# An attention and gMLP kernel: two attention products held at other places in VectorE's order

## The chip, the cores and the metric

The kernel runs on one core of a Trainium2 chip. The metric is the device time of one execution in microseconds (us), as the median of several runs. The engines of a core are TensorE (PE, matrix products; PEld is its loading of weights), VectorE (DVE), ScalarE (ACT), GpSimd (POOL) and SyncE (SP, which issues DMAs). Each runs its own instructions strictly in the order in which the built program lists them, and waits on semaphores where it needs another engine's result.

## The reference

The input x has 2048 rows of 512 numbers. Its normalised rows go through an attention branch and a gated MLP branch:

```
xn = layernorm(x)
# attention: 32 heads of 16, each row sees 8 rows at distance 0, 2, .. 14 behind it
q, k, v = split(xn @ wqkv)
s = softmax(q . k[i - 2w] / 4) weighted sum of v[i - 2w], heads joined, @ wo
# gMLP: 1792 hidden, halves of 896
z  = gelu(xn @ w_in);  z1 = z[:, :896];  z2 = layernorm(z[:, 896:])
g  = w_sp @ z2 + b_sp          # w_sp is 2048 x 2048, it mixes rows
b  = (z1 * g) @ w_out
out = x + s * silu(b)
```

All is float32. A float32 matrix product is done as three passes of a reduced type: every operand is split into a high part (a copy on ACT) and a low part (the difference, on DVE), and high x high, high x low and low x high are added up in PSUM.

## The kernel before, in words

On PE the work runs in stages, one behind the other: the q, k, v product (lines 385 to 387), z1 (703 to 705), z2 (730 to 732), the spatial product g (825), the projection with w_out (tiles b, 1066 to 1068), and the projection with wo (tiles s, the same lines). The trace shows these stages back to back from some 12 to 689 us.

The **spatial product** mixes rows with w_sp. It is computed by a scheme with seven block products on sums of blocks; `block_product` (848) runs one of them over eight steps, and in each step takes the next 128 x 512 mixing weight and multiplies it with up to four tiles of z2. The accumulators are the eight PSUM banks g_a_f. `plain` (859) hands out the weights that are blocks of w_sp as they stand, named wsp_c_js. Each is loaded, and then split by `split` (194): the high part on ACT at line 195, the low part on DVE at line 197. The list `lows` holds all low parts in the order in which they were written, so `lows[-1]` is the latest. In the names of the trace, wsp_1h is the high part of the second weight and wsp_1l its low part; the trace leaves the first number out. The banks g_1_f are first set to a bias by `seed` on ACT (line 843), behind a matmul at line 983.

In the **z2 stage**, the tiles zt come out of gelu on ACT (733). DVE takes their statistics (742, 743, 745), POOL raises the variance to the power -1/2 (746) and makes the negative shift nmz (748), and ACT normalises with it (754). DVE then forms differences and sums of the tiles (767), which the block products need, and splits them (197, tiles BIG<-zt).

The **attention** between the projections is done on DVE in 32 steps (16 units of rows and heads, two steps each), written as one chain in `attention`, lines 530 to 686. Each step has scores pr<-k,q (573), their sum over the head's 16 numbers, lg<-pr (580), the softmax (shift 598 to 601, exponential on ACT 606, norm 612 to 614), the **weighted product** pv<-v,lg (620), a first fold of it on POOL (633), two more folds and a transposition on DVE (638, 639, 646), and a store of the result to o_d by POOL's queue (647). POOL's queue also loads k, q and v. `line` (536) ties each DVE instruction of the attention to the one before it, so that their order among themselves never changes. The weighted products are kept in the list `sums_of` (628): the tenth is pv_4_4, the eleventh pv_5_0, and the twenty-fifth pv_12_0.

The order of the whole program is chosen when it is built: a scheduler goes through the program with a model of how long each instruction takes and always places what its model finds ready, the attention with a low priority (LOW, 532). Lines that call `add_manual_dep` with NOSYNC tie one instruction behind another in this order; they add no wait at run time. One such line stands in `plain`: when the weight wsp_0_6 is handed out, a weighted product is put behind its low part.

`wout` (1054) lists the seven split weights of w_out, wout_0 to wout_6. `upper_last` (961) evicts the last accumulators of g through the tiles yl, and `late` (930) loads and splits products stored earlier (tiles ul).

The attention's results come back from o_d into the tiles ol, are split (o_3h on ACT, o_3l on DVE), and multiplied with wo in the last stage; line 1117 is silu on tiles sg, line 1127 multiplies it with the result.

Of the kernel before, what the change touches and what calls it, by code (L numbers as in the profile page):

```python
# [52 lines left out]
NOSYNC = mybir.DependencyInfo(mybir.DependencyClass.NoSync, mybir.DependencyReason.DATA)  # L53
# [4 lines left out]
def kernel(  # L58
# [15 lines left out]
    lows, highs, sums_of = [], [], []  # L74
# [85 lines left out]
    def weight_pair(name):  # L160
        i = next(slot)
        return (
            wts.tile([P, 512], F32R, tag=f"whi{i}", name=name + "h"),
            wts.tile([P, 512], F32R, tag=f"wlo{i}", name=name + "l"),
        )

    def fetch(src, n, name):
        raw = raws.tile([P, 512], F32, tag="raw", name=name + "r", bufs=RAW)
        pin(nc.sync.dma_start(raw[:, :n], src))
        return raw  # L170
# [4 lines left out]
    def prep(src, n, name, raw=None, pair_=None):  # L175
        if raw is None:
            raw = fetch(src, n, name)
        hi, lo = pair_ or weight_pair(name)
        split(hi[:, :n], lo[:, :n], raw[:, :n])
        return hi, lo  # L180
# [13 lines left out]
    def split(hi, lo, src):  # L194
        first_ = pin(nc.scalar.activation(hi, src, AF.Copy))
        highs.append(first_)
        lows.append(pin(nc.vector.tensor_tensor(lo, src, hi.bitcast(F32), op=ALU.subtract)))
        return first_
# [94 lines left out]
    first = []  # L293
# [230 lines left out]
    def t4(name, n=2):  # L524
        t = wide.tile([P, 2 * CT], F32, tag="t4", name=name, bufs=WIDE)
        return t.rearrange("p (i t) -> p i t", i=2)[:, :n]
# [208 lines left out]
    def spatial_block(c, js):  # L735
        return prep(w_sp[c, js], CT, f"wsp_{c}_{js}")
# [95 lines left out]
    def z1_pair(c, f0, n):  # L832
        zl = t4(f"zl_{c}_{f0}", n)
        nc.sync.dma_start(zl, z1_d[f0 : f0 + n, c].rearrange("f p t -> p f t"))
        return zl
# [12 lines left out]
    def block_product(a, name, z, w, odd=None, start=False, stop=False, steps=()):  # L848
        for n, s0 in enumerate(range(0, HT, 2)):
            for s in (s0, s0 + 1):  # L850
                wp = w(s)
                for f in range(ODD):
                    three(banks[a, f], z(s, f), wp, start and s == 0, s == HT - 1, not start)
                if odd:
                    three(banks[a, ODD], odd(s), wp, False, s == HT - 1, True)
            for do in steps[n] if steps else ():
                do()

    def plain(a, c, r):
        def w(s):  # L860
            js = r * HT + s
            pair_ = spatial.get((2 * a + c, js)) or spatial_block(2 * a + c, js)
            if (a, c, js) == (0, 0, 6):
                tc.add_manual_dep(
                    sums_of[9].ins, lows[-1].ins.name, NOSYNC, reason="first weights ahead"
                )
            return pair_

        return w

    def summed(a, half_, i):
        return lambda s: prep(sums_d[a, half_, s, :, i], CT, f"ws_{a}{half_}{i}_{s}")
# [12 lines left out]
    def at(r, f0):  # L885
        return lambda s, f: z2_block(r * HT + s, f0 + f)
# [9 lines left out]
    def minus(out_, p_, q_):  # L896
        nc.vector.tensor_tensor(out_, p_, q_, op=ALU.subtract)
# [28 lines left out]
    def gated(c, f, src, zt):  # L926
        times(zt, src, zt)
        split(*ut_at(c, f), zt)
# [32 lines left out]
    def upper_last(a, f0, n):  # L961
        zl, yl = z1_pair(2 * a, LAST + f0, n), t4(f"yl_{a}_{f0}", n)
        nc.sync.dma_start(yl, y_d[a, f0 : f0 + n].rearrange("f p t -> p f t"))
        for f in range(f0, f0 + n):
            minus(yl[:, f - f0], banks[a, f], yl[:, f - f0])
            gated(2 * a, LAST + f, yl[:, f - f0], zl[:, f - f0])
# [85 lines left out]
    upper_last(0, 2, 1)  # L1052
    block_product(1, "m3b", at(1, LAST), summed(1, 1, 0))
    wout = [prep(w_out[:, f, :], D, f"wout_{f}") for f in range(FB)]
    upper_last(1, 0, 2)
    upper_last(1, 2, 1)
    for a in range(2):
# [120 lines left out]
```

## Time and profile before

| what | value |
|---|---|
| time, median of 3 runs (lowest, highest) | 695.79 us (694.64, 697.7) |
| the profiled execution's own time | 694.39 us |
| its span in the trace | 692.4 us |
| matmuls in the profiled execution | 3084 |
| bytes moved by DMA | 182.36 MB, mean 263 GB/s |

The profile is of one execution; its instructions span 692.4 us, and 1.99 us of the execution's own time lie around them. Here the busy share of PE and DVE in 40 equal slices of the span, in tenths (9 is 90% or more), and the clock granted to PE:

```profile
PE   8999999999999999999999999999999999999998
DVE  6677867999999979899999999999999999979775
PEclk9999999999999999999999999999999999999999
```

Both engines are busy nearly throughout. In rows of the timeline that follow below, the columns are the start, the duration, the engine, the line, the operation, result and operands, and in brackets the idle time before it and who ended it. In rows of groups they are the count, the busy time and the mean of one in ns, and the idle time before.

### The profile page before, as it was taken

How to read it: one execution, taken by the hardware profiler on the slowest of the kernel's cores; microseconds unless marked ns; L12 is line 12 of the kernel's file. 1: busy time of each engine (PE TensorE's matmuls, PEld its weight loads, DVE VectorE, ACT ScalarE, POOL GpSimd, SP SyncE). 2: the span in 40 equal slices, each digit the busy share in tenths (PEclk: the TensorE clock that was granted, in tenths of full speed). 3: DMA queues.
4: the chain of work that ended last, by engine and by line, in shares of the span. 5: the costliest groups of instructions: out<-in, count | busy, mean ns of one | idle time of the engine just before them, and what ended most of it. 6: DMA issues, size and time to landing. Idle time of an engine off the chain costs nothing.

```text
span 692.4 us, 9239 instructions
## 1 busy us (share of the span) xinstructions
PE 686.6 (99%) x3084; PEld 573.6 (83%) x3084; DVE 619.5 (89%) x866; ACT 278.6 (40%) x458; POOL 214.0 (31%) x242
## 2 busy tenths in 40 slices
PE   8999999999999999999999999999999999999998
PEld 7788888888888899987888888888888888888886
DVE  6677867999999979899999999999999999979775
ACT  3343233324324256765624544433344353211531
POOL 3104737282343321223223221223201202632320
PEclk9999999999999999999999999999999999999999
DMA  8769899969999865266998778776585791645896
GB/s 268 245 199 297 276 353 370 344 213 336 411 410 384 334 222 186 92 216 218 287 401 299 277 241 294 228 251 223 161 290 196 234 339 65 214 159 191 251 324 238
DMA packets 102223, 182.36 MB, mean 263 GB/s; under 512 B 9184, under 2 KB 45280, under 8 KB 102176
## 3 DMA queue, kind: packets, MB, share of 16 engines
q1 hardware_dynamic: 56624, 102.21, 44.2%
q0 software_dynamic: 13824, 52.24, 20.9%
q10 hardware_dynamic: 31728, 27.33, 11.7%
q8 instruction: 24, 0.39, 0.2%
q14 instruction: 23, 0.19, 0.1%
HBM read 122.42 MB, written 59.32 MB: 262 GB/s over the span
## 4 chain that ended last, share of the span: by engine, by line
PE 93%; DVE 2%; DMA 1%; ACT 1%; issue 1%; POOL 1%; SPq 0%; DVEq 0%; ACTq 0%
PE g L825 37%; PE qkv L385 6%; PE qkv L387 6%; PE qkv L386 6%; PE z L705 4%; PE z L703 4%; PE b L1068 4%; PE b L1066 4%; PE b L1067 4%; PE z L704 4%; PE z L732 3%; PE z L731 3%; PE z L730 3%; PE s L1068 2%; PE s L1067 2%; PE s L1066 2%
## 5 line engine op out<-in xcount | busy, mean ns | idle before, releaser
L633 POOL TENSOR_TENSOR pv<-pv 128x1024 f32<-128x1024 f32 x29 | 69.6, 2401 | 92.8 <-DVE pv L620 82.5
L573 DVE TENSOR_TENSOR pr<-k,q 128x2048 f32<-128x2048 f32 x32 | 73.6, 2299 | 4.3 <-DMA k<-qkv_d 4.1
L620 DVE TENSOR_TENSOR pv<-v,lg 128x2048 f32<-128x2048 f32 x32 | 74.5, 2329 | 0.6
L580 DVE TENSOR_REDUCE lg<-pr 128x128 f32<-128x2048 f32 x32 | 72.9, 2279 | 0.1
L647 POOL DMA_DIRECT2D o_d<-tt x32 | 18.0, 563 | 137.8 <-DVE tt L646 104.6
L433 ACT ACTIVATE stage<-qkv 128x512 f32<-128x512 f32 x40 | 23.0, 590 | 30.9 <-DMA qkv_d<-stage 21.0
L1077 ACT ACTIVATE bt<-b 128x512 f32<-128x512 f32 x16 | 9.6, 599 | 50.0 <-PE b L1068 45.8
L807 POOL DMA_DIRECT2D ol<-o_d x32 | 17.8, 556 | 36.2 <-DMA ol<-o_d 9.1
L709 ACT ACTIVATE z1t<-z 128x512 f32<-128x512 f32 x28 | 15.5, 596 | 27.5 <-DMA z_d<-z1t 14.5
L732 PE MATMUL z<-w_0h,BIG 128*128 128x512 f32 x64 | 25.0, 391 | 0.0
L731 PE MATMUL z<-w_0l,BIG 128*128 128x512 f32 x64 | 25.0, 391 | 0.0
L730 PE MATMUL z<-w_0h,BIG 128*128 128x512 f32 x64 | 24.9, 389 | 0.0
L742 DVE BATCH_NORM_STATS2 zst<-zt 128x6 f32<-128x448 f32 x32 | 19.3, 613 | 6.1 <-ACT zt L733 6.0
L754 ACT ACTIVATE zt<-zt,nmz,mvz 128x896 f32<-128x896 f32 x16 | 17.5, 1129 | 17.1 <-POOL nmz L748 17.1
L280 DVE TENSOR_TENSOR xT<-xT,mr 128x512 f32<-128x512 f32 x20 | 13.8, 688 | 11.8 <-DMA mr<-mv_d 6.8
L638 DVE TENSOR_TENSOR pv<-pv 128x512 f32<-128x512 f32 x32 | 22.9, 715 | 0.0
L732 PE MATMUL z<-w_1h,BIG 128*128 128x384 f32 x64 | 21.5, 336 | 0.0
L730 PE MATMUL z<-w_1h,BIG 128*128 128x384 f32 x64 | 21.5, 335 | 0.0
L731 PE MATMUL z<-w_1l,BIG 128*128 128x384 f32 x64 | 21.4, 335 | 0.0
L733 ACT ACTIVATE zt<-z 128x512 f32<-128x512 f32 (+1 forms) x32 | 15.9, 536 | 13.5 <-DMA sums_d<-sa 10.2
L552 POOL DMA_DIRECT2D k<-qkv_d x13 | 7.0, 536 | 43.8 <-DVE pr L573 43.8
L393 POOL TENSOR_TENSOR sb<-sa,sb 128x512 f32<-128x512 f32 x12 | 18.9, 1574 | 5.1 <-DMA sb<-in_w_sp 4.8
(478 smaller groups left out, 2256.9 us busy)
## 6 DMA issues: line engine op xcount, KB each, us to landing
qkv_d<-stage ACTq DMA_DIRECT2D x24, 512.0 KB
v<-qkv_d POOLq DMA_DIRECT2D x14, 704.0 KB, 5.1
k<-qkv_d POOLq DMA_DIRECT2D x13, 704.0 KB, 5.8
sums_d<-sa POOLq DMA_DIRECT2D x14, 512.0 KB, 7.9
sums_d<-sb POOLq DMA_DIRECT2D x14, 512.0 KB, 7.9
z_d<-z1t ACTq DMA_DIRECT2D x14, 512.0 KB
zl<-z_d SPq DMA_DIRECT2D x12, 512.0 KB
tr<-t_d SPq DMA_DIRECT2D x12, 384.0 KB
```

The lines of the kernel that those rows point to most:

```text
L385: nc.tensor.matmul(pq, xh[:, k], wh, start=k == 0, stop=False)
L386: nc.tensor.matmul(pq, xh[:, k], wl, start=False, stop=False)
L387: nc.tensor.matmul(pq, xl[:, k], wh, start=False, stop=k == KB - 1)
L573: line(nc.vector.tensor_tensor(pr, taps(ks[u], j0), qb.unsqueeze(1).to_broadcast([P, W, NJ * CS]), op=ALU.mult))
L580: line(nc.vector.tensor_reduce(lgs[u][:, j0 * HS : (j0 + NJ) * HS].rearrange("p i w -> p w i"), pr.rearrange("p w (i d) -> p w i d", d=DH) ...
L620: line(nc.vector.tensor_tensor(pv.rearrange("p w (i d) -> p w i d", d=DH), taps(vs[u], j0).rearrange("p w (i d) -> p w i d", d=DH), lgs[u] ...
L633: eng.tensor_tensor(pv[:, 0:4], pv[:, 0:4], pv[:, 4:8], op=ALU.add)
L730: nc.tensor.matmul(pz, xh[:, k], wh, start=k == 0, stop=False)
L731: nc.tensor.matmul(pz, xh[:, k], wl, start=False, stop=False)
L732: nc.tensor.matmul(pz, xl[:, k], wh, start=False, stop=k == KB - 1)
L825: nc.tensor.matmul(pg, z[a], w[b], start=start and i == 0, stop=stop and i == 2, skip_group_check=seeded)
L1066: nc.tensor.matmul(pp[:, cols], hi, wh, start=k == 0, stop=False)
```

## The change

Two numbers of the order are given. The hold in `plain` now takes the eleventh weighted product, `sums_of[10]`, in place of the tenth; the tenth may be placed anywhere that the chain of the attention allows. A new line behind the list `wout` puts the twenty-fifth, `sums_of[24]`, behind the low part of wout_6.

```diff
             if (a, c, js) == (0, 0, 6):
                 tc.add_manual_dep(
-                    sums_of[9].ins, lows[-1].ins.name, NOSYNC, reason="first weights ahead"
+                    sums_of[10].ins, lows[-1].ins.name, NOSYNC, reason="first weights ahead"
                 )
...
     wout = [prep(w_out[:, f, :], D, f"wout_{f}") for f in range(FB)]
+    tc.add_manual_dep(sums_of[24].ins, lows[-1].ins.name, NOSYNC, reason="output weights ahead")
     upper_last(1, 0, 2)
```

No instruction of the computation is added or taken away. What moves is where instructions stand. Lines behind 1054 have a number higher by one in the changed kernel.

The first place is on DVE, in the z2 stage, behind the statistics of the tile zt_9. So it stands in the changed kernel (pv_4_4 is the tenth product, v and lg its operands; mvz and zst are the statistics of z2's tiles; sr are sums of w_sp):

```order
L742 BN_STATS zst_9_2683<-zt_9_2552 128x6 x2
L620 TENSOR_TENSOR pv_4_4_1452<-v_2_0_1424,lg_4_1363 128x2048
L580 TENSOR_REDUCE lg_6_1444<-pr_6_0_1445 128x8x16
L743 BN_AGGR mvz_96<-zst_1_2679 128x2
L393 TENSOR_TENSOR sr_1_6_0_0r_2535<-sr_1_6_0_0r_2535,sr_1_6_1_8r_2541 128x512
L745 TENSOR_SCALAR mvz_96<-mvz_96 128x2
L742 BN_STATS zst_2_2779<-zt_2_2621 128x6
L743 BN_AGGR mvz_96<-zst_9_2683 128x2
L742 BN_STATS zst_2_2779<-zt_2_2621 128x6
L573 TENSOR_TENSOR pr_6_4_1457<-k_3_0_1440,q_3_0_1441 128x2048
```

In the kernel before, L743 of zst_1 follows L742 of zst_9 directly, and the tenth product stands some hundred rows later, in the stage of the spatial product, right behind the low part of wsp_0_6 and with the same L580 (lg_6<-pr_6_0) behind it. At that place the changed kernel has the eleventh product pv_5_0, with the sum lg_6<-pr_6_4 behind it. Of the steps between, L573 (pr_6_4), L638, L639, L646, L612, L613 and L614 have moved ahead into the z2 stage with the tenth product.

The second place is the hand-over from z2 to the spatial product, on DVE and on PE. On DVE, from the second half's statistics of the tile zt_6 up to the low part of the second mixing weight (the first number behind wsp is the block's, the second the step's; BIG is the store of the split z2), before:

```order
L742 BN_STATS zst_6_3123<-zt_6_2975 128x6
L197 TENSOR_TENSOR BIG_98<-zt_5_2889,BIG_98 128x4x128
L743 BN_AGGR mvz_96<-zst_6_3123 128x2
L767 TENSOR_TENSOR zt_5_2889<-zt_5_2889 128x384
L197 TENSOR_TENSOR BIG_98<-zt_13_2890,BIG_98 128x7x128
L742 BN_STATS zst_14_3127<-zt_14_2976 128x6
L767 TENSOR_TENSOR zt_5_2889<-zt_5_2889,zt_13_2890 128x384
L742 BN_STATS zst_7_3149<-zt_7_3059 128x6
L743 BN_AGGR mvz_96<-zst_14_3127 128x2
L197 TENSOR_TENSOR wsp_0_1l_3092<-wsp_0_1r_3089,wsp_0_1h_3091 128x512
```

In the changed kernel:

```order
L742 BN_STATS zst_6_3123<-zt_6_2975 128x6
L197 TENSOR_TENSOR BIG_98<-zt_4_2805,BIG_98 128x4x128
L743 BN_AGGR mvz_96<-zst_6_3123 128x2
L767 TENSOR_TENSOR zt_4_2805<-zt_4_2805 128x384
L767 TENSOR_TENSOR zt_4_2805<-zt_4_2805,zt_12_2806 128x384
L197 TENSOR_TENSOR BIG_98<-zt_12_2806,BIG_98 128x7x128
L742 BN_STATS zst_14_3127<-zt_14_2976 128x6
L197 TENSOR_TENSOR BIG_98<-zt_5_2889,BIG_98 128x4x128
L767 TENSOR_TENSOR zt_12_2806<-zt_12_2806,zt_4_2805 128x384
L742 BN_STATS zst_7_3149<-zt_7_3059 128x6
L743 BN_AGGR mvz_96<-zst_14_3127 128x2
L197 TENSOR_TENSOR wsp_0_1l_3092<-wsp_0_1r_3089,wsp_0_1h_3091 128x512
```

The combinations of z2's tiles are one tile further back: five of them (three of line 767, and the splits of 3 and of 7 blocks of zt_12 and zt_13) that stood ahead of the low part of wsp_0_1 before stand behind it now.

On PE, at the same hand-over, before:

```order
L825 MATMUL g_0_1_3190<-wsp_0_0h_2471,BIG_98 128x512
L825 MATMUL g_0_2_3193<-wsp_0_0h_2471,BIG_98 128x512
L825 MATMUL g_0_2_3193<-wsp_0_0l_2472,BIG_98 128x512
L825 MATMUL g_0_2_3193<-wsp_0_0h_2471,BIG_98 128x512
L825 MATMUL g_0_3_3194<-wsp_0_0h_2471,BIG_98 128x512
L825 MATMUL g_0_3_3194<-wsp_0_0l_2472,BIG_98 128x512
L825 MATMUL g_0_3_3194<-wsp_0_0h_2471,BIG_98 128x512
L825 MATMUL g_0_0_3189<-wsp_0_1h_3091,BIG_98 128x512
L825 MATMUL g_0_0_3189<-wsp_0_1l_3092,BIG_98 128x512
```

And in the changed kernel, from the same row on:

```order
L825 MATMUL g_0_1_3190<-wsp_0_0h_2471,BIG_98 128x512
L825 MATMUL g_0_0_3189<-wsp_0_1h_3091,BIG_98 128x512
L825 MATMUL g_0_1_3190<-wsp_0_1h_3091,BIG_98 128x512
L983 MATMUL g_1_0_3191<-BIG_98 128x512
L983 MATMUL g_1_1_3192<-BIG_98 128x512
L825 MATMUL g_0_0_3189<-wsp_0_1l_3092,BIG_98 128x512
```

The low part of the second weight, wsp_0_1l, is used three matmuls sooner, and the two matmuls of line 983, which come ahead of the seeds of the banks g_1, have moved up to this place.

The third place is on DVE, where the projection with w_out begins (yl, zl and ul are tiles of the gated product, wout_6l the last low part of w_out). Before:

```order
L197 TENSOR_TENSOR wout_6l_5338<-wout_6r_5335,wout_6h_5337 128x512
L614 TENSOR_TENSOR lg_12_1687<-lg_12_1687,sm_12_1750 128x256
L897 TENSOR_TENSOR yl_1_0_5343<-g_1_1_3192,yl_1_0_5343 128x512
L897 TENSOR_TENSOR yl_1_2_5355<-g_1_2_3195,yl_1_2_5355 128x512
L197 TENSOR_TENSOR BIG_98<-ul_1_0_5371,BIG_98 128x512 x2
L894 TENSOR_TENSOR zl_2_4_5341<-yl_1_0_5343,zl_2_4_5341 128x512
L197 TENSOR_TENSOR BIG_98<-ul_1_2_5377,BIG_98 128x512
L620 TENSOR_TENSOR pv_12_0_1754<-v_6_0_1748,lg_12_1687 128x2048
```

In the changed kernel:

```order
L197 TENSOR_TENSOR wout_6l_5338<-wout_6r_5335,wout_6h_5337 128x512
L897 TENSOR_TENSOR yl_1_0_5343<-g_1_1_3192,yl_1_0_5343 128x512
L197 TENSOR_TENSOR BIG_98<-ul_1_0_5371,BIG_98 128x512
L620 TENSOR_TENSOR pv_12_0_1754<-v_6_0_1748,lg_12_1687 128x2048
L580 TENSOR_REDUCE lg_13_1728<-pr_13_4_1741 128x8x16
```

The twenty-fifth product stands behind wout_6l in both; it has moved up to the third row behind it.

## The prediction

> **What bounds the kernel now.** First the busy time of each engine and the chain that ended last, both from the profile's page:
>
> ```profile
> span 692.4 us, 9239 instructions
> PE 686.6 (99%) x3084; PEld 573.6 (83%) x3084; DVE 619.5 (89%) x866; ACT 278.6 (40%) x458; POOL 214.0 (31%) x242
> PE 93%; DVE 2%; DMA 1%; ACT 1%; issue 1%; POOL 1%; SPq 0%; DVEq 0%; ACTq 0%
> ```
>
> TensorE (PE) is busy for 686.6 of 692.4 us and makes 93% of the chain. The matmuls are the same before and after. The change can therefore only win what PE loses by waiting, and can only cost what it makes PE wait. Next I read the list of PE's waits, which is complete in these four rows:
>
> ```profile
> PE warm L290 <- POOL ident masks.py:199: 1.4, 1, 1.4
> PE xt L228 <- DVE x L221: 0.3, 1, 0.3
> PE xt L228 <- DVE mvx L213: 0.3, 1, 0.3
> PE g L825 <- ACT g L843: 0.3, 1, 0.3
> ```
>
> Three are in the opening, long before the first product that moves. One is left, and the timeline of PE shows its size; the window behind it gives PE's pace (the columns are stretch, length, busy time with count for PE, PEld, DVE, ACT, POOL, then granted clock, DMA share, GB/s):
>
> ```profile
> 314.68 0.39 PE L825 MATMUL g<-wsp_6h,BIG 128*128 128x512 f32 x1
> 315.35 0.50 PE L825 MATMUL g<-wsp_0h,BIG 128*128 128x512 f32 x1 [0.28 <-ACT g L843]
> ...
> 315.68 0.39 PE L825 MATMUL g<-wsp_0l,BIG 128*128 128x512 f32 x1
> ...
> 316.00:570.00 254.00, 254.00 (x1122) 210.31 (x1121) 248.76 (x345) 110.82 (x184) 58.78 (x57) 1.00 0.78 265
> ```
>
> One matmul takes 254.00 / 1122 = 0.226 us, start to start. From 314.68 to 315.68 two starts took 1.00 us in place of 0.45, so this wait costs **0.55 us**. That is all that PE loses between the opening and its last matmul. The most that the change can bring is 0.55 us, 0.08%.
>
> **The change part by part: the first hold.** The instructions that move are attention work on VectorE (DVE). Their means, from the grouped instructions:
>
> ```profile
> L573 DVE TENSOR_TENSOR pr<-k,q 128x2048 f32<-128x2048 f32 x32 | 73.6, 2299 | 4.3 <-DMA k<-qkv_d 4.1
> L620 DVE TENSOR_TENSOR pv<-v,lg 128x2048 f32<-128x2048 f32 x32 | 74.5, 2329 | 0.6
> L580 DVE TENSOR_REDUCE lg<-pr 128x128 f32<-128x2048 f32 x32 | 72.9, 2279 | 0.1
> L638 DVE TENSOR_TENSOR pv<-pv 128x512 f32<-128x512 f32 x32 | 22.9, 715 | 0.0
> L639 DVE TENSOR_TENSOR pv<-pv 128x256 f32<-128x256 f32 x32 | 14.3, 446 | 0.3
> L646 DVE STREAM_TRANSPOSE tt<-pv 128x256 f32<-128x256 f32 x32 | 14.0, 437 | 0.5
> L614 DVE TENSOR_TENSOR lg<-lg,sm 128x256 f32<-128x256 f32 x16 | 7.4, 465 | 0.2
> L612 DVE TENSOR_REDUCE sm<-lg 128x32 f32<-128x256 f32 x16 | 6.0, 378 | 0.0
> L613 DVE RECIPROCAL sm<-sm 128x32 f32<-128x32 f32 x16 | 5.5, 347 | 0.2
> ```
>
> Both holds set an order and add no semaphore to wait for; behind the products on DVE stands whatever the order puts there. With the tenth product free, it and L580 stand in the z2 stage, and L573, L638, L639, L646, L612, L613 and L614 follow before z2 ends. One each of the nine is 9.70 us by these means. Neighbours overlap by about 0.08 us (below, L620 starts at 573.65 and L580 behind it at 575.85: 2.20 of its 2.28), so nine cost some 9.0 us. At the old place the eleventh product and an L580 of the same sizes stand now, so there nothing changes.
>
> What these 9.0 us can delay is the hand-over from z2 to the spatial product, where PE needs the low part wsp_1l of the second mixing weight. DVE's timeline there, the window over the z2 stage from the new place to that low part, and PE's first use:
>
> ```profile
> 290.28 0.63 DVE L742 BATCH_NORM_STATS2 zst<-zt 128x6 f32<-128x448 f32 x1 [2.73 <-ACT zt L733]
> ...
> 291.42 0.20 DVE L743 BATCH_NORM_AGGREGATE mvz<-zst 128x2 f32<-128x12 f32 x1
> 291.53 0.55 DVE L767 TENSOR_TENSOR zt<-zt 128x384 f32<-128x384 f32 x1
> 292.01 1.08 DVE L197 TENSOR_TENSOR BIG<-zt,BIG 128x896 fp32r<-128x896 f32 x1
> ...
> 294.65 0.64 DVE L197 TENSOR_TENSOR wsp_1l<-wsp_1r,wsp_1h 128x512 fp32r<-128x512 f32 x1
> ...
> 247.00:295.30 48.30, 48.30 (x241) 43.43 (x240) 40.34 (x88) 35.40 (x56) 9.58 (x18) 1.00 0.48 158
> ...
> 297.89 0.39 PE L825 MATMUL g<-wsp_1l,BIG 128*128 128x512 f32 x1
> ```
>
> The order postpones five z2 instructions behind wsp_1l: four like the one at 291.53 (0.48 to the next start) and one like that at 292.01 (1.08, less the overlap 1.00), 2.9 us. DVE has 9.0 - 2.9 = **6.1 us** more to do ahead of wsp_1l. Its idle time in this window is 48.30 - 40.34 = **7.96 us**, and the slack behind is 297.89 - 295.29 = 2.60 us; since PE's order now asks for wsp_1l three matmuls sooner (0.68), 1.92 are left.
>
> The two ends: if none of the idle time takes up work, wsp_1l comes 6.1 later and PE waits 6.1 - 1.92 = 4.2 us. If enough does, DVE has caught up at 290.28, where it now waits 2.73 us for an eviction of the tile zt_6 that PE's pace sets. From there to wsp_1l the new order has twice an L742 and a split of 512 columns (1.14 a pair, 290.28 to 291.42), one more L742 (0.62, less the overlap 0.54), two L743 (0.11 each), a split of 1.00 and three L767 of 0.48: in all 5.48 us in place of 294.65 - 290.28 = 4.37. With its own 0.64, wsp_1l is ready at 296.40, and PE asks for it at 297.89 - 0.68 = 297.21. That is 0.81 us early. The rest of the 6.1, 6.1 - 1.11 = 5.0 us, has to fit into 7.96 us of idle time, all of it ahead of 290.28. I take this end, since all nine moved instructions stand ahead of that point, and put 0.3 us of waiting into the sum, because 0.81 is little.
>
> The moved steps also queue work on POOL and ScalarE (ACT). Their rows at the old place, and what ACT waited for from 235 to 320:
>
> ```profile
> 304.34 2.40 POOL L633 TENSOR_TENSOR pv<-pv 128x1024 f32<-128x1024 f32 x1 [6.47 <-DVE pv L620]
> 306.69 0.65 POOL L562 DMA_DIRECT2D v<-qkv_d  x1
> ...
> 304.40 1.28 ACT L606 ACT_TABLE_LOAD   x1
> ...
> ACT zt L754 <- POOL nmz L748: 17.1, 6, 6.0
> ACT wsp_3h L195 <- PE g L983: 4.1, 1, 4.1
> ```
>
> On POOL the fold L633 of the tenth product and the load of the next v (2.40 + 0.65 = 3.05 us) now stand ahead of the L746 and L748 that make nmz for z2's second tiles; the store of o_d and the loads of k and q follow between such pairs. On ACT one exponential and two table loads of 1.28 us come in between the evictions, 2.6 us and a little. Bounds: nothing, if they fall into ACT's 48.30 - 35.40 = 12.9 us of idle time in the window, or 3.05 us, if all of nmz's delay reaches the evictions; that is inside the 4.2 above. I take nothing: 12.9 is four times either of them. No load on SyncE's queue moves by more than a few rows.
>
> ACT's wait at wsp_3h is why the seed was late at 314.71: it stands behind wsp_3h and two more high parts. In the new order the seeds g_1 stand ahead of wsp_2h to wsp_5h, so **-0.55 us** goes in full. What is late next there is nothing that I found: DVE has 9 us less to do between 300 and 335.
>
> [...]
>
> ```profile
> 277.09 0.70 POOL L746 TENSOR_TENSOR mvz<-mvz,nhalf 128x2 f32<-128x2 f32 x1 [8.41 <-DVE mvz L745]
> 317.35 1.08 POOL L746 TENSOR_TENSOR mvz<-mvz,nhalf 128x2 f32<-128x2 f32 x1 [2.44 <-DVE mvz L745]
> ```
>
> The same small operation takes 0.70 us at one place and 1.08 at the other, 0.38 more, whatever DVE does beside it. [...]
>
> **The second hold.** The twenty-fifth product, the low part that it is to follow, and PE's first use of that part:
>
> ```profile
> 569.11 0.68 DVE L197 TENSOR_TENSOR wout_6l<-wout_6r,wout_6h 128x512 fp32r<-128x512 f32 x1
> ...
> 573.65 2.28 DVE L620 TENSOR_TENSOR pv<-v,lg 128x2048 f32<-128x2048 f32 x1
> 575.85 2.28 DVE L580 TENSOR_REDUCE lg<-pr 128x128 f32<-128x2048 f32 x1
> ...
> 575.92 0.39 PE L1067 MATMUL b<-wout_6l,BIG 128*128 128x512 f32 x1
> ```
>
> The product stands behind wout_6l already. The hold keeps that, though the product has moved up: it now stands three rows behind wout_6l, not seven, at about 570.4. PE uses wout_6l eight matmuls sooner, 575.92 - 8 x 0.226 = 574.11, and it is there at 569.79: slack 4.3 us. What the product and its L580 (4.4 us) now stand ahead of, an eviction of yl, a gated low part of ul and three zl, is for later quarters of the output projection. **Cost 0.** Without the hold the product would have stood ahead of some wout low parts, 4.4 us, about the slack.
>
> **The tail.** The attention's end is the tightest row there:
>
> ```profile
> 677.58 0.69 DVE L197 TENSOR_TENSOR o_3l<-ol,o_3h 128x512 fp32r<-128x512 f32 x1 [3.63 <-ACT o_3h L195]
> ...
> 679.74 0.39 PE L1068 MATMUL s<-BIG,o_3l 128*128 128x512 f32 x1
> ```
>
> It is ready at 678.27, 1.47 us early. Steps that come sooner lengthen this; a longer slack wins nothing.
>
> **The sum**, against the profiled execution: 694.39 (span 692.4 and 1.99 around it) - 0.55 + 0.3 = 694.14. The median of the runs, 695.79, is 1.40 above it, so I forecast 695.54 for the median, rounded to **695.5 us**.
>
> **The rivals.**
>
> *No effect.* The second hold names an order that already held; if the first only exchanges products and the seed still comes late, the time is 695.8. For it: the gain is one wait of 0.28 us. Against it: nine instructions move. Chance 0.09.
>
> *The hand-over pays, and the time is slower.* The fold and the products in the z2 stage stand ahead of nmz, nmz comes late, ACT stands at L754 with gelu evictions and wsp highs behind it, and PE waits for a bank or for wsp_1l. It decides from the point where wsp_1l comes more than 1.92 us later than now. With no idle time usable: + 4.2 - 0.55 = +3.65, 699.4. If the postponed 2.9 us do not help either: 9.0 - 1.92 - 0.55 = +6.5, 702.3. For it: ACT's 17.1 us of waiting for nmz, and that the hand-over is left with 0.81 us even if DVE catches up. Against it: the gap at 290.28, which alone takes up 2.73. Chance 0.14.
>
> The granted clock is 1.00 in every window above, with 0.28 us of waiting. [...]
>
> *The tail turns late.* If the last unit came later by one product and its fold (2.28 + 0.72 = 3.0), o_3l would be 3.0 - 1.47 = 1.5 us late: 697.3. Against it: the steps come sooner. Chance 0.05.
>
> **How the numbers follow.** The forecast has 0.72, no effect 0.09, tail 0.05, hand-over 0.14. About 0.5%, 3.5 us, is what a measurement of this kernel can tell from no change. Faster by more would need over six times what PE loses: 0.02, for an unlucky set of runs. Within: 0.70 + 0.09 + 0.05 = 0.84. Slower: 0.14. The range goes from the fastest run less 0.55, 694.1, down to 694.0 by rounding, up to the slower rival's 699.4.
>
> **What would show it.** Right: PE's list of waits has no seed at the start of the second spatial product; wsp_1l is ready near 296.4, before PE asks for it; the tenth product stands near 247 us, the twenty-fifth near 570; DVE's idle time between 247 and 295 has shrunk from 8 to about 2 us. Wrong: a PE wait at 295 to 300 for wsp_1l or for a bank in z2, a PE wait for a wout low part near 569 to 574, or a later o_3l. A slower kernel without a PE wait would refute the whole approach.

## The result, and the profile after

The changed kernel took 701.23 us (median of 6 runs, 699.0 to 702.58) beside 696.0 us for the kernel before on the same chip: a ratio of 1.007 with a 95% interval of 1.0046 to 1.0094. It is slower, by about 5 us, where 695.5 was forecast with a range up to 699.4. The profiled execution took 699.65 us, 5.26 more than the one before. Two later series of the same kernel, r1 and r3 below, gave 1.0049 (1.0031 to 1.0068) and 1.0043 (1.0025 to 1.0061), so the slowdown is real; the intervals of the three series overlap. One execution of all that follow, in experiment s1, took 1410.66 us, with matmuls 0.44 us apart in place of 0.23; no wait is read from its trace.

The page of the changed kernel: span, busy time of each engine, and the chain that ended last.

```profile
span 697.6 us, 9233 instructions
PE 688.9 (99%) x3084; PEld 573.9 (82%) x3084; DVE 619.1 (89%) x866; ACT 277.9 (40%) x460; POOL 220.2 (32%) x242
PE 47%; DVE 23%; DMA 20%; issue 6%; ACT 2%; POOL 2%; SPq 0%; DVEq 0%; POOLq 0%; ACTq 0%
```

The matmuls are the same 3084, DVE has the same work, and POOL is busy 6.2 us longer for the same operations. PE's share of the chain fell from 93% to 47%: the chain leaves PE at o_3h (684.03 below) and follows DVE's attention back. PE's waits, the longest first (line, who released it, total, times, longest):

```profile
PE z L730 <- ACT zt L733: 2.9, 1, 2.9
PE warm L290 <- POOL ident masks.py:199: 1.3, 1, 1.3
PE xt L228 <- DVE mvx L213: 0.5, 1, 0.5
PE qkv L308 <- ACT BIG L229: 0.2, 1, 0.2
```

The wait for the seed (L825 behind L843) is gone, as forecast. A new one has come in the z2 stage: PE waits for ACT to evict an accumulator. Its timeline around it, of all engines that have a part in it (start, duration, engine, line, operation, in brackets the idle time before and its releaser):

```profile
267.41 0.69 DVE L393 TENSOR_TENSOR sr_8r<-sr_0r,sr_8r 128x512 f32<-128x512 f32 x1 [2.04 <-DMA sr_8r<-in_w_sp]
...
272.51 0.16 DVE L745 TENSOR_SCALAR mvz<-mvz 128x2 f32<-128x2 f32 x1
272.58 1.09 DVE L197 TENSOR_TENSOR BIG<-zt,BIG 128x896 fp32r<-128x896 f32 x1
272.75 3.48 POOL L746 TENSOR_TENSOR mvz<-mvz,nhalf 128x2 f32<-128x2 f32 x1 [7.06 <-DVE mvz L745]
...
275.59 0.62 DVE L742 BATCH_NORM_STATS2 zst<-zt 128x6 f32<-128x448 f32 x1
276.33 0.70 POOL L748 TENSOR_SCALAR nmz<-mvz 128x1 f32<-128x1 f32 x2
276.83 2.16 ACT L754 ACTIVATE zt<-zt,nmz,mvz 128x896 f32<-128x896 f32 x2 [3.88 <-POOL nmz L748]
278.03 0.39 PE L732 MATMUL z<-w_0h,BIG 128*128 128x512 f32 x1
278.89 1.87 ACT L195 ACTIVATE BIG<-zt 128x512 fp32r<-128x512 f32 x3
280.67 1.81 ACT L733 ACTIVATE zt<-z 128x512 f32<-128x512 f32 x4
281.30 0.50 PE L730 MATMUL z<-w_0h,BIG 128*128 128x512 f32 x1 [2.88 <-ACT zt L733]
...
282.33 0.63 PE L731 MATMUL z<-w_0l,BIG 128*128 128x512 f32 x1
282.75 0.63 PE L732 MATMUL z<-w_0h,BIG 128*128 128x512 f32 x1
...
285.74 0.34 PE L730 MATMUL z<-w_1h,BIG 128*128 128x384 f32 x1
```

This is read from the bottom up. PE stops at 278.03 and starts again at 281.30, because its accumulator is evicted at 280.67 only. That eviction (L733) stands on ACT behind the normalisation L754 and three splits. L754, for the tiles zt_3 and zt_11, waited 3.88 us for nmz. And nmz waits for POOL's power L746, two numbers per partition, which takes 3.48 us. In the kernel before, the power of the same pair is this row of POOL's timeline, with the DVE rows beside it:

```profile
266.95 0.56 DVE L767 TENSOR_TENSOR zt<-zt 128x384 f32<-128x384 f32 x1
267.08 0.99 POOL L746 TENSOR_TENSOR mvz<-mvz,nhalf 128x2 f32<-128x2 f32 x1 [0.93 <-DVE mvz L745]
268.62 0.63 DVE L742 BATCH_NORM_STATS2 zst<-zt 128x6 f32<-128x448 f32 x1 [1.11 <-ACT zt L733]
```

So the power starts 5.67 us later and lasts 2.49 longer: it ends 8.16 us later. Of the 5.67, 1.00 was there ahead of the change's place: the last DVE instruction ahead of it, L742 of zst_9, starts at 247.44 in place of 246.44. The other 4.67 come by DVE's 9 us of attention, less what was postponed and what idle time took up. Nearly all the idle time that is left there is the wait of 2.04 us for the load of sr_8r. PE waits 3.04 us, so some 5.1 us were there as slack, and without the longer power about 0.55 us of waiting would have been left. Behind the wait the matmuls start 0.43 apart instead of 0.23. From 278.03 to 285.74 PE does 13 matmuls of 0.228 in 7.71 us: 4.75 lost, 3.04 by the wait and most of the rest by the half rate. In the windows the granted clock is the third number from the end:

```profile
247.00:295.30 48.30, 45.42 (x215) 39.82 (x214) 43.23 (x86) 27.88 (x43) 19.43 (x23) 0.96 0.57 189
278.90:282.31 3.41, 1.01 (x4) 0.86 (x5) 2.77 (x6) 3.41 (x8) 0.00 (x0) 1.00 0.99 355
282.31:285.72 3.41, 3.41 (x9) 2.63 (x8) 3.41 (x8) 1.56 (x4) 0.00 (x0) 0.50 0.64 217
```

The first row is the window that the forecast used: DVE's idle time there went from 7.96 to 5.07 us, POOL's busy time from 9.58 to 19.43. The other two are the stretch in which PE waited and the one in which it ran at half the clock. Some 1 us more is lost at the end, at two uses of the last part, o_3h and o_3l. The later of them on PE, and the split that goes with it on DVE:

```profile
683.53 0.39 PE L1069 MATMUL s<-BIG,o_2l 128*128 128x512 f32 x1
684.03 0.50 PE L1067 MATMUL s<-BIG,o_3h 128*128 128x512 f32 x1
684.01 0.69 DVE L197 TENSOR_TENSOR o_3l<-ol,o_3h 128x512 fp32r<-128x512 f32 x1 [3.45 <-ACT o_3h L195]
```

The account: + 4.75 - 0.55 (seed) + 1.0 (o_3h) = 5.2, and the spans differ by 697.6 - 692.4 = 5.2 us.

### The profile page after: what moved, and what is told of

Its sections match the earlier page's. It is cut to its first block, busy times and chain, and to the rows that moved or that the text cites. A ratio compares the mean times of both kernels' runs of the same rounds, so it can differ in the third digit from the quotient of the medians.

```text
span 697.6 us, 9233 instructions
## 1 busy us (share of the span) xinstructions
PE 688.9 (99%) x3084; PEld 573.9 (82%) x3084; DVE 619.1 (89%) x866; ACT 277.9 (40%) x460; POOL 220.2 (32%) x242
## 4 chain that ended last, share of the span: by engine, by line
PE 47%; DVE 23%; DMA 20%; issue 6%; ACT 2%; POOL 2%; SPq 0%; DVEq 0%; POOLq 0%; ACTq 0%
PE g L825 39%; DMA ol<-o_d 5%; DVE lg L580 4%; DVE pr L573 3%; DMA qkv_d<-stage 3%; DVE pv L620 3%; DMA sb<-in_w_sp 2%; PE qkv L308 2%; DMA sums_d<-sb 2%; DMA xT<-in_x_t 1%; DMA o_d<-tt 1%; DVE xT L280 1%; DMA mr<-mv_d 1%; DVE BIG L234 1%; DVE pv L638 1%
## 5 line engine op out<-in xcount | busy, mean ns | idle before, releaser
L573 DVE TENSOR_TENSOR pr<-k,q 128x2048 f32<-128x2048 f32 x32 | 73.6, 2300 | 4.6 <-DMA k<-qkv_d 4.4
L620 DVE TENSOR_TENSOR pv<-v,lg 128x2048 f32<-128x2048 f32 x32 | 74.5, 2329 | 0.5
L580 DVE TENSOR_REDUCE lg<-pr 128x128 f32<-128x2048 f32 x32 | 72.9, 2280 | 0.1
L754 ACT ACTIVATE zt<-zt,nmz,mvz 128x896 f32<-128x896 f32 x16 | 17.7, 1132 | 17.1 <-POOL nmz L748 17.0
L638 DVE TENSOR_TENSOR pv<-pv 128x512 f32<-128x512 f32 x32 | 22.8, 714 | 0.0
L733 ACT ACTIVATE zt<-z 128x512 f32<-128x512 f32 (+1 forms) x32 | 15.6, 536 | 17.7 <-DMA sums_d<-sa 12.0
L746 POOL TENSOR_TENSOR mvz<-mvz,nhalf 128x2 f32<-128x2 f32 x8 | 11.4, 1430 | 33.5 <-DVE mvz L745 33.5
L197 DVE TENSOR_TENSOR BIG<-zt,BIG 128x512 fp32r<-128x512 f32 (+2 forms) x24 | 18.5, 775 | 3.8 <-ACT BIG L195 3.8
L393 POOL TENSOR_TENSOR sb<-sa,sb 128x512 f32<-128x512 f32 x12 | 18.8, 1565 | 4.4 <-DMA sb<-in_w_sp 4.1
```

Of the source, the lines that this page charges most:

```text
L393: eng.tensor_tensor(out_, p_, q_, op=ALU.add)
L573: line(nc.vector.tensor_tensor(pr, taps(ks[u], j0), qb.unsqueeze(1).to_broadcast([P, W, NJ * CS]), op=ALU.mult))
L580: line(nc.vector.tensor_reduce(lgs[u][:, j0 * HS : (j0 + NJ) * HS].rearrange("p i w -> p w i"), pr.rearrange("p w (i d) -> p w i d", d=DH) ...
L620: line(nc.vector.tensor_tensor(pv.rearrange("p w (i d) -> p w i d", d=DH), taps(vs[u], j0).rearrange("p w (i d) -> p w i d", d=DH), lgs[u] ...
L638: line(nc.vector.tensor_tensor(pr[:, 0:2], pr[:, 0:2], pr[:, 2:4], op=ALU.add))
```

## The experiments

**The theory** is the chain above: the tenth product in the z2 stage puts DVE's statistics late against PE, POOL's power is held up beside DVE, and ACT keeps finished accumulators waiting behind L754. **The rivals**: the second hold costs the time, at wout or at the tail; or POOL has no part in it, and DVE's 9 us alone make nmz late. Open beside that was what the half rate costs, and from which wait.

**e1 and r2: the first hold alone.** The new line behind `wout` is left out. (The second hold alone needs no run: it gives the order of the kernel before on every engine, row for row.)

```diff
-    tc.add_manual_dep(sums_of[24].ins, lows[-1].ins.name, NOSYNC, reason="output weights ahead")
```

> The first hold moved, the second line left out. Up to the output projection its instructions stand as in the changed kernel; behind it the 25th product stands ahead of the low parts of w_out. Theory A (the tenth product in the z2 stage makes the loss): PE waits 2.5 to 3.3 us for an eviction near 278 us and then runs some 3 us at half rate, so it is slower than before by 4 to 7 us, 700 to 703. Rival C (the second hold makes the loss): within 1 us of before, no PE wait in z2.

> The first hold alone once more, on the same chip. Its instructions up to the output weights stand as in the changed kernel, so both have the same z2 order. A2: a PE wait of 0.9 to 3 us at L730 and none at the end; 1 to 3 us above before. D: within 1 us of before.

e1 took 696.93 us (10 runs), ratio 1.0016 (0.9993 to 1.0038); r2 697.17 us (12 runs), 1.0033 (1.0017 to 1.0049). PE's waits of r2 behind the opening:

```profile
PE z L730 <- ACT zt L733: 1.5, 1, 1.5
PE g L825 <- DVE wsp_1l L197: 0.4, 1, 0.4
PE s L1066 <- ACT o_3h L195: 0.2, 1, 0.2
```

The stall in z2 belongs to the first hold. It is shorter than in the profile above (1.0 in e1), and no half rate follows in either (the clock granted over the span is 0.999 in both, and the matmuls behind the wait start 0.23 apart in e1). Neither expectation for e1 holds as it stands: the wait is less than half of the 2.5 to 3.3 us, and no half rate and no 700 us came, but the wait that its rival excluded is there. By its times alone e1 can't be told from the kernel before; r2 can. Without the second hold the twenty-fifth product stands at 563.16 (e1) and 565.42 (r2), 8 to 10 us ahead of the kernel before (573.65), and o_3h is in time or almost.

**r1 and r3: the changed kernel again**, on the chips of r2 and of s1.

> The changed kernel once more, beside the next two on one chip. Theory A2 (two losses: one at a bank in z2, whose size goes with the moment at which VectorE enters z2, and about 1 us at the last o_3 parts, which only the second hold brings): PE waits at L730 for an eviction again, 0.9 to 3 us, and loses 0.5 to 1.5 us at the last o_3h and o_3l; its median is 1 to 2 us above the kernel with the first hold alone. Theory D (the second hold makes nearly all of the loss): its median is 3.5 us or more above that kernel's on this chip too, with more than 2 us of PE waiting behind 568 us.

> The changed kernel once more beside the reordered one on one chip. Power of the third pair 3.48 us as in its two earlier profiles; TensorE's wait in the second gating is 0 where the tenth product begins at 245.1 us or before, and grows by about 1 us for each us that it begins later, to 2.9 at 248.0; over 2.5 us the matmuls behind it run at half rate. Time 1.003 to 1.009 of the kernel before.

r1 took 697.78 us (6 runs), r3 697.0 (8 runs), with the ratios given above. r1's median is 0.6 us above r2's on the same chip, where its expectation had 1 to 2 us, and its rival, for which the second hold makes nearly all of the loss, 3.5 or more. PE's waits of r3 behind the opening, and the two rows from which the stall is read:

```profile
PE s L1067 <- ACT o_3h L195: 0.9, 1, 0.9
PE z L730 <- ACT zt L733: 0.4, 1, 0.4
PE g L825 <- DVE wsp_1l L197: 0.4, 1, 0.4
...
269.94 3.48 POOL L746 TENSOR_TENSOR mvz<-mvz,nhalf 128x2 f32<-128x2 f32 x1 [6.95 <-DVE mvz L745]
278.49 0.50 PE L730 MATMUL z<-w_0h,BIG 128*128 128x512 f32 x1 [0.45 <-ACT zt L733]
```

The same program has 0, 0.4 and 2.9 us of this wait in its three profiles. Over the five profiles of the two kernels that have this order in z2, in us:

| run | tenth product starts on DVE | POOL's power L746 starts | lasts | PE's first matmul behind the wait | from L746 to it |
|---|---|---|---|---|---|
| r1 | 245.14 | 268.85 | 3.48 | no wait | |
| r3 | 245.26 | 269.94 | 3.48 | 278.49 | 8.55 |
| e1 | 246.31 | 270.31 | 3.48 | 278.86 | 8.55 |
| r2 | 246.87 | 270.89 | 3.48 | 279.44 | 8.55 |
| changed, first profile | 247.96 | 272.75 | 3.48 | 281.30 | 8.55 |

From the start of the power to PE's matmul it is 8.55 us each time. PE asks at 277.7 to 278.3 in all of them. So every us by which DVE comes later to this place is paid in full on PE, and at 2.9 the half rate comes on top. In the kernel before the power starts at 267.08, ahead of all of these.

Why DVE comes at 245 in one execution and at 248 in another no experiment tells, but the traces show a part of it: waits for loads. Of the 2.82 us between r1 and the first profile at the tenth product, 1.84 are there at 119 us already, and most of the rest is a wait of 0.91 us for a load of sb at 202.34, which r1 does not have (r2 has 2.20 there). From the tenth product to the power it is 23.71 us in r1 and 24.79 in the first profile; the difference, 1.08, is that of their waits for the load of sr_8r, 0.96 and 2.04.

r1 has no wait in z2, and its span is still 2.0 us above the one before (694.4 and 692.4). Its PE loses 0.4 us at wsp_1l, 0.7 at wout_4h and wout_4l, and 1.2 at o_3h and o_3l, against the 0.5 that it gains at the seed. So the stall in z2 is not all of the slowdown: the rest is work that DVE brings late to the hand-over, to w_out and to the tail.

The second hold moves the twenty-fifth product back to 575.09 in r1, and in r1 and r3 the wait for o_3h is 0.9 where r2 has 0.2 and e1 none. On one chip, r1 has 1.0049 and r2 1.0033; their intervals overlap, so that the second hold costs time is seen in the traces, and not shown by the times.

**e3 and e4: the power and the shift on DVE**, in the changed kernel (e3) and in the kernel before (e4), so that POOL has no part in the chain.

```diff
-        nc.gpsimd.tensor_tensor(rstd, rstd, nhalf.to_broadcast([P, 2]), op=ALU.pow)
+        nc.vector.reciprocal(rstd, rstd)
         for j in (i, HT + i):
-            nc.gpsimd.tensor_scalar(
+            nc.vector.tensor_scalar(
```

> The changed kernel with the z2 statistics' power and shift (lines 746 and 748) taken from POOL to VectorE, so that no POOL operation stands in the chain from statistics to normalisation; the power is replaced by a reciprocal, so z2 is scaled by 1/variance in place of its root. The tenth product stays at its row in the z2 stage. Theory A (POOL's L746 took 3.48 us because VectorE's two-input instructions shut it out): the PE wait of 2.9 us near 278 goes or falls under 0.5 us, no half rate, 694 to 697. Rival B (the 4.4 us of the product and of L580 ahead of the statistics make nmz late, POOL or not): PE still waits 2 us or more in z2, 699 to 702.

> The kernel before with the same edit (statistics on VectorE, reciprocal for the power). It prices the edit by itself: both theories expect no PE wait in z2 and a time within 1.5 us of before, 694.5 to 697.5; if it is slower by more, the edit costs something of its own.

e3 took 701.08 us, ratio 1.0084 (1.0058 to 1.011); e4 703.18 us, 1.01 (1.0072 to 1.0128). e3's tenth product starts at 247.21, a time at which the table lets one expect 1.5 to 2.9 us, and its list of waits has none in z2. Behind the opening it has 2.3 us at o_3h, 0.7 at wout_4h, 0.4 at wsp_1h, and 0.2 each at wout_4l and wsp_1l.

With POOL out of the chain the stall in z2 is gone, though the product stands in the stage. But the pair fails as an experiment on the time, and both miss the times expected of them: the edit gives the scheduler other costs, it places much of the rest otherwise, and e4, which was to be a control, loses 2.8 us at o_3h, then runs some matmuls at half rate (starts 0.43 apart from 688.66 on), and ends 8.4 us behind its last matmul, where the kernel before takes 3.5. The time of e3 says nothing of the change.

**s1 and s2: one instruction in another place.** In all five profiles of the table the power ends within 0.05 us of the end of the first one-input instruction that DVE runs behind L745 (here L742 at 275.59 + 0.62 = 276.21, the power at 276.23); all between them (L197, L393, L767) have two inputs. (That it need not be a one-input instruction is shown below, with e5.) In s1 and s2 that L742, of zst_4, comes right behind L745 of zt_3 and zt_11 (the third pair of the expectations, counted from 0), and five two-input instructions behind it; up to there the order is that of the changed kernel.

```diff
+                one = nc.vector.bn_stats(st[:, h], zt[:, h * FQ : (h + 1) * FQ])
+                if (j, h) == (4, 0):
+                    for late in (lows_of[10], odd_of[0], combined[0][3], combined[2][0], done[-2]):
+                        tc.add_manual_dep(late.ins, one.ins.name, NOSYNC, reason="one input first")
```

> The changed kernel with one reordering on VectorE: the first statistics instruction of zst_4 (one input) comes right behind the addition of EPS for the third pair (L745 of the changed kernel) and five two-input instructions that stood between come behind it. Theory (GpSimd's power waits until VectorE's first one-input instruction behind a run of two-input ones): the power that took 3.48 us ends within 0.2 us of the end of that statistics instruction, so it lasts 0.7 to 1.1 us, the normalisation on ScalarE comes 2.4 us sooner after the addition, and TensorE's wait in the second gating (L730 there) is 0 for an entry of the tenth product before 247.5 us, and at most 0.5 us for one at 248; kernel 1 to 3 us faster than the changed kernel on the same chip where that one waits. Rival (the length of the power has another cause, such as GpSimd's own sequencer or the eviction beside it on ScalarE): the power stays near 3.5 us and the wait is the one of the changed kernel, about the tenth's entry less 245.2 us.

> The same reordered kernel again, since the first profile fell on an execution of twice the time (1410 us, every matmul about three times as long), in which no wait can be read. As before: if the power waits for VectorE's first one-input instruction, the third pair's power ends within 0.2 us of the end of the first statistics of zst_4, lasts 0.7 to 1.1 us in place of 3.48, and TensorE's wait in the second gating is 0 for an entry of the tenth product before 247.5 us; if it has another cause the power stays near 3.5 us and the wait is the entry less about 245.1 us. The first series gave 699.6 us against 697.0 for the changed kernel on that chip, so a later wait has to show that makes up for it, of 2 to 3 us at the spatial weights or the last o_3h, since from VectorE's row 310 on the order is another one.

s1 took 699.62 us in the median; without the execution named above its ratio is 1.0074 (1.0051 to 1.0098). s2 took 698.1 us (5 runs), ratio 1.0041 (1.0027 to 1.0055). The 1 to 3 us by which s1 was to be faster than the changed kernel did not come. The place in s2's timeline (lines behind 393 have other numbers there: L750 for L745, L744 for L742, L751 for L746), and PE's waits behind the opening:

```profile
271.61 0.16 DVE L750 TENSOR_SCALAR mvz<-mvz 128x2 f32<-128x2 f32 x1
271.70 0.63 DVE L744 BATCH_NORM_STATS2 zst<-zt 128x6 f32<-128x448 f32 x1
271.86 0.70 POOL L751 TENSOR_TENSOR mvz<-mvz,nhalf 128x2 f32<-128x2 f32 x1 [7.04 <-DVE mvz L750]
273.34 2.21 ACT L759 ACTIVATE zt<-zt,nmz,mvz 128x896 f32<-128x896 f32 x2 [1.29 <-POOL nmz L753]
...
PE g L833 <- ACT g L851: 2.0, 2, 1.3
PE g L833 <- ACT wsp_1h L195: 1.0, 1, 1.0
PE s L1075 <- ACT o_3h L195: 0.3, 1, 0.3
PE b L1076 <- DVE wout_4l L197: 0.2, 1, 0.2
```

The power took 0.70 us in place of 3.48. The normalisation starts 1.73 us behind the L745 of its pair, where the changed kernel needs 276.83 - 272.51 = 4.32. PE does not wait in z2, though the power starts at 271.86, between r2 (1.5 us of waiting) and the changed kernel's first profile (2.9). This is shown, then: with the statistics in place of two-input instructions beside it, POOL's small operation took 0.70 us in place of 3.48, and most of the stall went with that. The time gains nothing by it. The order behind that place is another, and 1.10 + 1.35 + 1.72 us at three starts in place of 0.23 each, about 3.5 us, are lost at the seeds and at wsp_1h: the expected later wait.

**e6 and e7: the tenth product elsewhere in z2**, behind the statistics of the tiles zt_3 and zt_11 (e6, i = 3), or of zt_6 and zt_14 (e7, i = 6).

```diff
-        nc.vector.tensor_scalar(rstd, rstd, EPS, None, op0=ALU.add)
+        added = nc.vector.tensor_scalar(rstd, rstd, EPS, None, op0=ALU.add)
+        if i == 3:
+            tc.add_manual_dep(sums_of[9].ins, added.ins.name, NOSYNC, reason="behind the statistics")
```

> The changed kernel with the tenth product held behind the fourth pair's statistics of z2, so that it stands at row 306 of VectorE, not at 269; both holds of the change stay. A2: the wait at L730 depends on what stands beside POOL's L746, so it is smaller, 0 to 1.5 us, and the loss at the end stays, 0.5 to 1.5 us; 1 to 3 us above before. D: as the changed kernel, 4 us or more above before.

> The same with the tenth product behind the seventh pair's statistics: it stands behind the low part of wsp_0_1, out of z2, and nothing of the attention is added to the z2 stage; both holds of the change stay. A2: no PE wait at L730 at all; what is left is the loss at the end, so 0.5 to 2 us above before. D: 4 us or more above before, all of it behind 568 us.

e6 took 701.79 us, ratio 1.0095 (1.007 to 1.012); e7 697.11 us, 1.0043 (1.0024 to 1.0061). No wait in z2 is left in either. Against the kernel before on their chip e6 is 7.5 us slower, where 1 to 3 was expected, and e7 2.8, where it was 0.5 to 2. e6's seed comes late instead, and PE runs at half rate behind it (starts 0.43 apart):

```profile
294.26 0.69 PE L985 MATMUL g<-BIG 128*128 128x512 f32 x2
298.34 0.79 PE L827 MATMUL g<-wsp_0h,BIG 128*128 128x512 f32 x1 [3.39 <-ACT g L845]
298.93 0.63 PE L827 MATMUL g<-wsp_0l,BIG 128*128 128x512 f32 x1
```

Behind that e6 waits 1.2 us at wout_6h and 2.5 at o_3h, with half rate once more (the clock granted over its span is 0.993). In e7 the seed is 2.3 us late and o_3h 0.6, without half rate (1.00). With the product later in z2 PE pays at the stage's end instead: at none of the three places tried were these 9 us free. No run here beats the kernel before, and at most 0.55 us was to be had.

**e5: the two prices by themselves**, in a kernel of its own: POOL's power beside runs of 1 to 6 DVE instructions of 512 columns with two inputs or with one, or of statistics; and runs of 60 matmuls, with waits of growing length between them.

> A small kernel that computes none of the reference; its output is zeros and rows of one product. Part one: a POOL power of 128x2 is released by a small VectorE instruction, behind which VectorE runs 1, 2, 3, 4 or 6 instructions of 128x512 with two inputs, or with one input, or statistics, and then three statistics. Theory A: beside two-input runs POOL's power ends only with the run, so about 1.0 us at 1 and 3.5 to 4.3 us at 6; beside one-input runs and statistics 0.7 to 1.1 us for every length. Rival B: 0.7 to 1.1 us everywhere. Part two: runs of 60 matmuls behind PE gaps of about 1 to 7 us. If a gap of 2.9 us is what halved the clock, gaps from about 3 us on are followed by some 3 us of matmuls at 0.43 us and shorter ones are not; if the threshold is 3.4 us or more, gaps of 3 us leave the rate at 0.23.

The power took 1.06 us at the head of a two-input run of whatever length, 0.79 to 0.96 beside one input, and 0.69 beside statistics; two of its rows:

```profile
37.34 1.06 POOL L114 TENSOR_TENSOR v_two<-v_two,half__72 128x2 f32<-128x2 f32 x1 [4.53 <-DVE v_two L109]
108.59 0.69 POOL L114 TENSOR_TENSOR v_stat<-v_stat,half__72 128x2 f32<-128x2 f32 x1 [5.27 <-DVE v_stat L109]
```

So its time did not grow with the run there, from 1 to 6 instructions, as the rival expected. The 3.48 us were not reproduced. s2's trace has both: 3.81 us at 300.88, again up to the end of DVE's first statistics, and 1.08 at 315.05, in the middle of a two-input run. Beside a single product L620 of 2.28 us the power took 2.67 us (e6 at 265.48, e7 at 295.71).

One reading goes through all of these rows: a power at whose start DVE runs a two-input instruction ends 0.55 to 0.58 us behind the end of such an instruction. In the first profile that is the last of five, L767, which starts at 275.12 and ends at 275.67, against 276.23 for the power; in e5 it is the first of the run; in the kernel before it is the L767 that ends at 267.51, against 268.07, and DVE stood idle there until 268.62. So in these rows the power's end keeps that distance to a two-input instruction, whether a one-input instruction follows or not; the statistics last 0.62 us, which is why their end falls on the same time. Why it is the first two-input instruction at some places and the last of five at another is open.

On the clock: PE idle for 1.35 us never led to half rate. 2.07 us did in one of two cases, 2.67 in one of two, and 3.4 us and more did in all 14. The starts behind it are 0.43 apart, in place of 0.23. The two rounds with 2.07 us, the first without half rate, the second with it, each with windows of 3.41 us around it:

```profile
38.36 0.50 PE L133 MATMUL pg<-xh,open 128*128 128x512 f32 x1 [2.08 <-ACT open L131]
37.22:40.63 3.41, 2.27 (x10) 1.89 (x11) 3.41 (x7) 1.05 (x2) 1.06 (x1) 1.00 0.00 0
...
240.78 0.50 PE L133 MATMUL pg<-xh,open 128*128 128x512 f32 x1 [2.07 <-ACT open L131]
238.60:242.01 3.41, 1.34 (x6) 1.05 (x6) 0.00 (x0) 1.86 (x3) 0.00 (x0) 1.00 0.00 0
242.01:245.42 3.41, 3.41 (x9) 2.64 (x8) 0.00 (x0) 0.00 (x0) 0.00 (x0) 0.50 0.00 0
```

These windows are not chosen freely. In every trace here the half clock comes in stretches of 3.41 us or a multiple (but for one that the trace's end cuts off), and all of a trace begin on one grid of 3.41 us. What tells the two rounds apart is PE's busy time in the stretch ahead. With 1.34 us, 39%, the clock fell to half for the next one; with 2.27, where the same wait lies across two stretches, it did not. Over all these traces but s1's, from 8 us on, full clock was followed by half where PE was busy for at most 43% of a stretch (22 times), and never where it was busy for 45% or more. So in these traces the length of a wait alone does not tell: r3's expectation, half rate behind more than 2.5 us, does not hold for one of the two waits of 2.67, and the 3.4 us that e5's expectation sets against 2.9 are not where it begins, since one wait of 2.07 us led to it.

The stall of 2.88 us in the first profile lies in the range in which both happen: it left PE 1.01 of 3.41 us busy, 30%, and the half clock began at 282.31, 1.0 us behind PE's new start. r2's wait of 1.51 us left 56%.

## Why the prediction was wrong, point by point

- **The seed's 0.55 us is "all that PE loses between the opening and its last matmul", and goes "in full"**: right. No profile of the changed kernel has that wait.
- **"I take nothing: 12.9 [us of ACT's idle time] is four times either of them"**: this step failed. ACT's idle time in the window is mostly its own waiting for nmz (17.1 us from 235 to 320 before, a row that the prediction quotes). While it waits there, the evictions behind it in order wait too (in the changed kernel L754 at 276.83, then three splits, then L733 at 280.67). Idle time that stands ahead of a waiting instruction takes up nothing that comes through that instruction. The bound of 3.05 us was too low as well: it had POOL's queue in it, and not that DVE's own statistics come late, 4.67 us by the change. Behind the start of the power, PE's matmul followed at 8.55 us, us for us.
- **"0.70 us at one place and 1.08 at the other, 0.38 more, whatever DVE does beside it"**: the second failure, and the size. The power of this pair went from 0.99 to 3.48, 2.49 us more. The two rows of before, 0.70 and 1.08, were no bound, since neither of them stood in front of this run of DVE's: the 0.70 at 277.09 has DVE's statistics beside it (276.91 to 277.53), the 1.08 at 317.35 one split with two inputs (317.17 to 317.85). What DVE does beside it is what told: 0.70 in s2, with the statistics beside it, against 3.48. The 2.2 us products are not what held this power; it was a row of short sums and splits, and beside a single product the power took 2.67 us (e6 and e7). The 1.06 us of e5, beside runs of 1 to 6 two-input instructions, do not explain 3.48.
- **"0.3 us of waiting into the sum", for wsp_1l**: about right. e1, r1, r2 and r3 lose 0.4 to 0.6 us there, start for start; in the first profile PE is late enough for it.
- **The second hold, "Cost 0."**: by itself right, since it gives the order that already was. But it was not weighed together with the first: without it the twenty-fifth product comes at 563 to 565 us, some 10 us sooner. The 4.3 us of slack were read from the order before; in r1 the low part wout_4l starts on DVE at 570.88 in place of 564.98, and PE loses 0.7 us there. "Near 570" for the product's start was wrong too: 577.31 in the first profile, and 575.09 in r1, where PE did not wait in z2.
- **"Steps that come sooner lengthen this", the slack of o_3l**: failed. The last transposition of the attention starts at 666.12 in place of 661.50, later by slightly more than PE (4.2 us behind the z2 stage), and o_3h costs 1.0 to 1.2 us in all three profiles. The attention was ahead up to the twenty-fourth product (539.48 in place of 544.99) and had lost this at the twenty-fifth. In r1 the last transposition is at 662.97, later too, without a stall in z2.
- **The rival "the hand-over pays"**, with a chance of 0.14, named the place: nmz late, ACT at L754 with evictions behind it, PE waiting for a bank, 3.65 to 6.5 us. The first series lies in it, r1 and r3 just below (+ 3.4 and + 3.1 us). It was put low because DVE could catch up at 290.28; PE's bank was needed at 278, ahead of that gap. The forecast and its range have no term for the half rate, which cost some 1.7 us (4.75 - 3.04) behind the wait of 2.88.

Left open: what makes DVE come to z2 up to 2.8 us later in some executions, beyond the loads named above, and with it why the first series is 2 us slower than r1 and r3 against their own controls; and why POOL's power ends behind one two-input instruction at some places (1.06 us in e5) and behind several at others (3.48 us).

## What to carry to other kernels

Before moving work into a stage, follow the chain that frees its accumulators through every engine, and compare it with the time at which PE asks, at each turn of the stage and not at its end alone. Idle time of an engine is worth something only where nothing that is late itself stands behind it: most of ScalarE's 12.9 us here was its own waiting for nmz. A small GpSimd step in such a chain should stand beside VectorE work like the statistics here (0.70 us, against 3.48 beside two-input instructions); and a reordering found in one execution should be tried over several, since the slack here was smaller than the difference between executions (2.8 us at the tenth product).

## What the runs showed of the hardware that was not expected

A GpSimd operation on two numbers per partition took 0.69 us beside VectorE's statistics, 1.06 us beside two-input instructions in e5, and 2.61 to 3.81 us beside some runs of these in the kernels; beside two-input instructions it ended each time 0.55 to 0.58 us behind the end of one. In these traces TensorE's clock fell to half in stretches of 3.41 us on a fixed grid, 22 times, each behind a stretch in which it was busy for at most 43%, and never behind one with 45% or more; waits of 2.07 us led to it in one case of two, and behind the wait of 2.88 us it came 1.0 us after TensorE had started again. Two executions of one program differed by 2.8 us in the time at which VectorE reached the same instruction (245.14 and 247.96), with nothing changed.
